# The first group's back product by seven products too, with the outputs of a chain left in its bank

## The chip, the cores and the metric

The kernel runs on one NeuronCore of a Trainium2 chip. The metric is the device time of one execution in microseconds; lower is better. Before the change three runs gave 863.26, 864.15 and 864.43 us, median 864.15. Engines: TensorE (PE) multiplies, ScalarE (ACT) copies and splits, VectorE (DVE) adds and subtracts, GpSimd (POOL) and SyncE (SP) issue transfers.

## What is computed

Three stages on 2304 tokens of 512 features, in float32:

```
x = attention(q, k, v)            # chunks of 64 tokens, 8 heads of 64
h = x @ w_in                      # 512 x 2048
y = (h * sigmoid(h)) @ w_out      # 2048 x 512      first MLP
a, b = y @ w_a, y @ w_b           # 512 x 1536      gated MLP
return (a * b) @ w_o2             # 1536 x 512
```

## The kernel before

**Precision.** [...] A product takes three passes: high by high, high by low, low by high. To split, ACT copies (the high part) and DVE subtracts (the low part).

**First MLP.** The weights come in a packed form and are unpacked in the course of the kernel. Blocks of 512 tokens go through 16 steps m of 128 hidden features. A step issues 12 matmuls of the next step's front (128x512), then 12 of its own back. SiLU runs on ACT, which writes `g` and its high part `ghi`; DVE makes `glo` (L409), which the back's third, sixth, ... matmul reads.

**Gated MLP.** Its tokens are three groups ("pairs") of two times T = 384. The front products are made by seven block products instead of eight (Strassen's scheme in Winograd's form): the weights' blocks are added and subtracted beforehand (`comb_sums`, L497: three DVE instructions) and split. One *unit* is one of the two matrices at one of STEPS = 6 steps: 7 products of 6 matmuls 128x384 each, gathered into four outputs. Pair 0 takes the combined weights while they are made: `make_half` (L522) splits products 0 to 3 of a unit (1024 wide) and 4 to 6 (768 wide) into a *ring* of 7 slots, from which they also leave for memory as `wg`. Later pairs read them back (`feed`, L553). `freed` or `refill` makes or fetches the next half when a half has been used.

The back by w_o2 is done by seven products in pairs 1 and 2, with combinations of w_o2 (`comb_load_2`, `comb_split_2`, L474 to L493). They are made once, four in the last A block (the steps of `W2_AT`) and two in pair 1, and are kept in memory as `w2`. In pair 0 the back is plain: 216 matmuls 128x512 (`back_b`, L694), three quarters of them in blocks of nine or twelve between the front products, with w_o2 split and stored high/low in the first MLP and loaded back by 24 transfers (`load_o2`, L1044).

**Order.** Every engine works its instructions in the order in which the program is written; there is no scheduler. Tiles come from pools with a fixed number of slots. The pool `big` has MA + 4 = 20 slots of 8 KB a partition and serves weights, ring, `buf` (loaded weights before their sums), `hl` (split combinations of w_o2 before they are written) and others; an instruction that writes a tile waits until the last reader of its slot is done, a transfer too. `in_last` (L1057) puts the work on weights into the 16 steps of the last A block, at two places of each ("c" and "c2"), ahead of that step's `glo`. `load_pair` (L587) brings y back for the operands of the next pair; for pair 0 that stands in step 5 of the last A block.

A chain of pair 0 (`chain`, L642) leaves its banks by four copies on ACT and four adds on DVE (`evacuate`, L1238, in the later pairs).

Of the kernel before, what the change touches and what calls it, by code (L numbers as in the profile page):

```python
# [20 lines left out]
P = 128  # L21
# [3 lines left out]
def chunk_attention_silu_mlp_gated_mlp(  # L25
# [10 lines left out]
    out: bass.AP,  # L36
# [26 lines left out]
    DM = out.shape[1]  # L63
# [57 lines left out]
    o2 = {}  # L121
# [67 lines left out]
    def upper():  # L189
        if not stage_1:  # L190
            return
        dest, w, sg, _ = stage_1.pop()
        nc.vector.scalar_tensor_tensor(  # L193
            out=w, in0=w, scalar=2.0**-20, in1=sg, op0=ALU.mult, op1=ALU.mult
        )
        if dest[0] == "f":
            wf[dest[1:]] = d = dram.tile([P, DM], F32, name=f"wf{dest[1]}{dest[2]}")
            leaving.append((d, w))
            return
        if dest[0] == "a":  # L200
            _, m, j = dest
            if m not in slots_a:
                slots_a[m] = slot("wA").rearrange("p (j n) -> p j n", j=4)
            hl = slots_a[m][:, 2 * j:2 * j + 2]
        else:
            wf[2, dest[1]] = d = dram.tile([P, DM], F32, name=f"wf2{dest[1]}")
            leaving.append((d, w))
            hl = late["conv"].tile([P, 2, DM], F32R, tag="hl", name="hl", bufs=1)
        nc.scalar.activation(hl[:, 0], w, AF.Copy)  # L209
        stage_2.append((dest, hl, w))  # L210

    def lower():
        if not stage_2:
            return
        dest, hl, w = stage_2.pop()
        nc.vector.tensor_tensor(out=hl[:, 1], in0=w, in1=hl[:, 0].bitcast(F32), op=ALU.subtract)
        if dest[0] == "a":
            wA.setdefault(dest[1], {})[dest[2]] = hl[:, 0], hl[:, 1]
        else:
            o2[dest[1]] = d = dram.tile([P, 2, DM], F32, name=f"wo{dest[1]}")  # L220
            leaving.append((d, hl.bitcast(F32)))
# [241 lines left out]
    def comb_load(u):  # L463
# [6 lines left out]
        for m, sl in ((2 * s, slice(1, 3)), (2 * s + 1, slice(0, 8, 4))):  # L470
# [3 lines left out]
    def comb_load_2(s):  # L474

        buf = slot("buf", F32).rearrange("p (o n) -> p o n", o=8)
        for h in range(2):
            nc.gpsimd.dma_start(out=buf[:, 1 - h], in_=wf[2, 2 * s][:, h * H:(h + 1) * H])
        nc.gpsimd.dma_start(
            out=buf[:, 2:6:2], in_=wf[2, 2 * s + 1].rearrange("p (o n) -> p o n", o=2)  # L480
# [16 lines left out]
    def comb_sums(u):  # L497
        summed.add(u)
        a21, a11, a12, s1, a22, s2, s4, s3 = (bufs[u][:, o] for o in range(8))
        nc.vector.tensor_tensor(out=s3, in0=a21, in1=a11, op=ALU.subtract)  # L500
        nc.vector.tensor_tensor(
            out=bufs[u][:, 3:6:2],
            in0=bufs[u][:, 0:8:7],
# [43 lines left out]
    for p in range(PAIRS):  # L547
        base.append(len(feeds))
        feeds += [wg[n] for n in range(2 * UNITS)]
        if p:  # L550
            feeds += [w2[:, n:min(n + 4, OPS * STEPS)] for n in range(0, OPS * STEPS, 4)]
# [11 lines left out]
    def chunk():  # L563
        u, o = divmod(used[0], OPS)
        h = int(o >= HALVES[1][0])
        return ring[2 * u + h][:, o - HALVES[h][0]]

    owed = [0]

    def chunk_done():  # L570
        used[0] += 1
        if used[0] % OPS in (0, HALVES[1][0]):
            owed[0] += 1
# [10 lines left out]
    pieces = []  # L584
# [16 lines left out]
    def operands(p):  # L601
# [4 lines left out]
        def take(o):  # L606
            if o not in xo:
# [3 lines left out]
                pieces.append(t[:, 2 * n:])  # L611
# [11 lines left out]
        def sub(dst, a, b):  # L623
# [4 lines left out]
            hi(0, b11), hi(5, b22), lo(0, b11), hi(1, b21), sub(t1, b12, b11),  # L628
            lo(5, b22), hi(2, t1), sub(t3, b12, b22), lo(1, b21), hi(6, t3), lo(2, t1),
            sub(t2, b22, t1), hi(4, t2), lo(6, t3), sub(t4, b21, t2), hi(3, t4),  # L630
            lo(4, t2), lo(3, t4),
        ]


    o2_at = {}
    gT2 = []

    order = ["at", "sB", "sA", "mm", "acc3"]

    held = []  # L640

    def chain(ct, filler):  # L642

        u0, u1, u2, u3, u4 = order
        order[:] = [u4, u1, u3, u2, u0]
        x1, x2, x3, x4 = (bank(t, [P, T]) for t in (u0, u2, u1, u3))

        def prod(ps, o, first):
            whi, wlo = (chunk()[:, i] for i in range(2))
            xhi, xlo = xo[o]  # L650
            for j, (a, b) in enumerate(((whi, xhi), (whi, xlo), (wlo, xhi))):
                for kk in range(KH):
                    nc.tensor.matmul(  # L653
                        ps,
                        lhsT=a[:, kk * P:(kk + 1) * P],
                        rhs=b[:, kk, :],
                        start=(first and j == 0 and kk == 0),
                        stop=(j == 2 and kk == KH - 1),
                        skip_group_check=True,
                    )  # L660
            chunk_done()

        def add(c, ps):
            nc.vector.tensor_tensor(out=ct[:, c], in0=ps, in1=ct[:, c], op=ALU.add)

        def keep(c, ps):
            nc.scalar.activation(ct[:, c], ps, AF.Copy)

        prod(x1, 0, True)
        keep(0, x1)  # L670
        prod(x3, 1, True)
        add(0, x3)
        refill()
        prod(x2, 2, True)
        keep(3, x2)
        prod(x4, 3, True)
        keep(2, x4)
        while held:
            held.pop()()
        yield  # L680
        prod(x1, 4, False)
        keep(1, x1)
        prod(x2, 5, False)
        add(1, x2)
        refill()
        yield
        filler()
        prod(x1, 6, False)
        add(2, x1)
        add(3, x1)  # L690

    accs = {}

    def back_b(t, m, ghi, glo, tag=None):  # L694

        if m == 0:
            accs[t] = bank(tag or f"acc{t}", [P, DM])
        whi, wlo = o2_at[m]
        for i, (g, w) in enumerate(((ghi, whi), (ghi, wlo), (glo, whi))):
            nc.tensor.matmul(  # L700
                accs[t],
                lhsT=g,
                rhs=w,
                start=(m == 0 and i == 0),
                stop=(m == MB - 1 and i == 2),
            )

    def store(p, t, by_act, halves=False):
        st = spool.tile([P, DM], F32, tag="tmp", name="ost", bufs=3)
        ps = accs.pop(t)  # L710
        if halves:
            nc.scalar.activation(st[:, :H], ps[:, :H], AF.Copy)
            nc.vector.tensor_copy(st[:, H:], ps[:, H:])
        elif by_act:
            nc.scalar.activation(st, ps, AF.Copy)
        else:
            nc.vector.tensor_copy(st, ps)
        r = (2 * NTB * p + t) * P
        (nc.scalar if by_act and not halves else nc.sync).dma_start(out=out[r:r + P, :], in_=st)

    g1 = {}

    def first_block(m0, mi):

        ghi, glo = g1.pop((m0, mi))
        for t in range(NTB):
            cols = slice(t * P, (t + 1) * P)
            back_b(t, m0 + mi, ghi[:, cols], glo[:, cols])

    def gate(ca, cb, s, c):  # L730

        m0, mi, second = 2 * s, c // 2, c % 2
        m = m0 + mi
        dst = gT2[m // 4][:, m % 4] if second else cb[:, c]
        nc.vector.tensor_tensor(out=dst, in0=ca[:, c], in1=cb[:, c], op=ALU.mult)

        def split():
            ghi = gpool.tile([P, T], F32R, tag="ghi", name="ghi")
            glo = gpool.tile([P, T], F32R, tag="glo", name="glo")
            nc.scalar.activation(ghi, dst, AF.Copy)  # L740
            nc.vector.tensor_tensor(out=glo, in0=dst, in1=ghi.bitcast(F32), op=ALU.subtract)
            g1[m0, mi] = ghi, glo

        return split

    def second_split(t, k, in_gpool):

        if in_gpool:
            hl = [gpool.tile([P, 4, P], F32R, tag=tg, name=tg) for tg in ("ghi", "glo")]
        else:  # L750
            if "gsp" not in late:
                late["gsp"] = spool.tile([P, 2, 2 * DM], F32R, tag="raw", name="gsp", bufs=1)
            half = late["gsp"][:, turn[0] % 2].rearrange("p (t m n) -> p t m n", t=2, m=4)
            turn[0] += 1
            hl = [half[:, 0], half[:, 1]]
        src = gT2[k][:, :, t * P:(t + 1) * P]
        nc.scalar.activation(hl[0], src, AF.Copy)
        nc.vector.tensor_tensor(out=hl[1], in0=src, in1=hl[0].bitcast(F32), op=ALU.subtract)
        return hl

    def second_back(t, k, hl, tag):
        for i in range(4):
            back_b(NTB + t, 4 * k + i, hl[0][:, i], hl[1][:, i], tag)
# [4 lines left out]
    for s in range(STEPS):  # L768
        for mat in range(2):
            units_b += [("f", mat, 2 * s), ("f", mat, 2 * s + 1), ("o", 2 * s + mat)]  # L770
# [20 lines left out]
    def prep_b():  # L791
        if done[1] < len(units_b):
            dest = units_b[done[1]]
            src = w_o2[dest[1]] if dest[0] == "o" else (w_a, w_b)[dest[1]][dest[2]]
# [15 lines left out]
    with tc.manual_schedule():  # L810
# [221 lines left out]
        o2_slots = []  # L1032
# [10 lines left out]

        def load_o2(m):  # L1044
            o2_at[m] = []
            for i in range(2):
                if not pieces and len(o2_slots) < 4:
                    o2_slots.append(slot("wo2"))
                    pieces.extend(o2_slots[-1][:, j * DM:(j + 1) * DM] for j in range(4))
                if pieces:  # L1050
# [448 lines left out]
```

## Time and profile before

| | |
|---|---|
| Median of three runs | 864.15 us |
| Profiled execution | 863.38 us |
| Its span, first to last instruction | 861.6 us |
| PE busy | 851.5 us (99%) |
| DVE busy | 588.7 us (68%) |
| ACT busy | 434.9 us (50%) |
| Granted clock of TensorE | 1.000 |

The span is what the trace covers; 1.8 us of the execution lie outside it. Durations are read from one execution, times of day in the trace count from the span's start. In a timeline a row "x6" is six instructions on end; the start of the next row less its own start is what a product takes, since matmuls overlap at their ends.

### The profile page before, as it was taken

The numbers are of one execution on the slowest core, as the hardware profiler recorded it, in microseconds if no ns is written. First come the engines' busy times: TensorE is split into PE (matmuls) and PEld (weight loads), VectorE is DVE, ScalarE is ACT, GpSimd is POOL, SyncE is SP. The second block draws the span as 40 slices with busy tenths as digits, with TensorE's granted clock in tenths as the row PEclk, the third lists the DMA queues.
The fourth block names the chain that finished last, engine by engine and source line by source line (L and its number), as shares of the span: only waits on it lengthen the run. The fifth ranks groups of instructions, "written<-read, shape, count | busy, mean of one in ns | idle before, by whom it ended". The sixth has DMA issues, their size and how long they took to land.

```text
span 861.6 us, 14197 instructions
## 1 busy us (share of the span) xinstructions
PE 851.5 (99%) x5448; PEld 767.9 (89%) x5448; DVE 588.7 (68%) x1143; ACT 434.9 (50%) x817; POOL 50.3 (6%) x91
## 2 busy tenths in 40 slices
PE   7999999999999999999999999999999999999998
PEld 7788888887888878888889999988999999999997
DVE  6997977757776577657575877445677686566663
ACT  6767766746664666544445443333334363333252
POOL 0000000020000000032200110000000000000000
PEclk9999999999999999999999999999999999999999
DMA  7354444266655665476984986654688887877751
GB/s 270 124 183 130 153 135 131 79 219 218 219 187 184 231 203 207 167 245 220 391 352 158 404 339 246 221 196 147 245 333 324 331 300 256 283 255 255 289 190 56
DMA packets 57347, 195.44 MB, mean 227 GB/s; under 512 B 6272, under 2 KB 12928, under 8 KB 50112
## 3 DMA queue, kind: packets, MB, share of 16 engines
q1 hardware_dynamic: 49632, 170.54, 55.0%
q0 software_dynamic: 6928, 22.81, 8.0%
q10 hardware_dynamic: 720, 1.18, 0.4%
q8 instruction: 43, 0.70, 0.3%
q14 instruction: 24, 0.20, 0.1%
HBM read 136.31 MB, written 58.20 MB: 226 GB/s over the span
## 4 chain that ended last, share of the span: by engine, by line
PE 97%; ACT 1%; DVE 1%; DMA 1%; SPq 0%; issue 0%; DVEq 0%; ACTq 0%
PE ps_acc L431 21%; PE ps_acc L1233 15%; PE ps_mm L392 15%; PE ps_sA L392 7%; PE ps_at L1233 7%; PE ps_acc L700 5%; PE ps_sA L1233 4%; PE ps_sB L653 2%; PE ps_sA L653 2%; PE ps_at L653 2%; PE ps_sB L1233 2%; PE ps_mm L1233 2%; PE ps_acc L653 2%; PE ps_sA L431 2%; PE ps_mm L653 1%; PE ps_sB L431 1%
## 5 line engine op out<-in xcount | busy, mean ns | idle before, releaser
L431 PE MATMUL ps_acc<-ghi,wA 128*128 128x512 f32 x512 | 159.9, 394 | 0.0
L1233 PE MATMUL ps_acc<-xo,ring 128*128 128x384 f32 x582 | 111.5, 334 | 0.0
L431 PEld LDWEIGHTS ps_acc<-ghi,wA 128*128 128x128 f32 x512 | 93.8, 188 | 19.2
L1233 PEld LDWEIGHTS ps_acc<-xo,ring 128*128 128x128 f32 x582 | 101.9, 188 | 0.0
L392 PE MATMUL ps_mm<-xhi,wA 128*128 128x512 f32 (+1 forms) x400 | 100.7, 373 | 0.0
L431 PE MATMUL ps_acc<-glo,wA 128*128 128x512 f32 x256 | 100.0, 391 | 0.0
L392 PEld LDWEIGHTS ps_mm<-xhi,wA 128*128 128x128 f32 x400 | 70.5, 188 | 12.6 <-ACT wA L209 0.2
L412 ACT ACTIVATE g<-ps_mm 128x512 f32<-128x512 f32 (+1 forms) x50 | 28.0, 560 | 86.7 <-PE ps_mm L392 81.7
L409 DVE TENSOR_TENSOR glo<-g,ghi 128x512 fp32r<-128x512 f32 x80 | 50.5, 632 | 19.1 <-ACT ghi L413 19.1
L1246 ACT ACTIVATE gq<-ps_acc 128x384 f32<-128x384 f32 x56 | 27.6, 492 | 60.2 <-PE ps_acc L1233 57.5
L431 PEld LDWEIGHTS ps_acc<-glo,wA 128*128 128x128 f32 x256 | 48.0, 188 | 10.3
L153 ACT ACTIVATE e<-e,ebias 128x512 uint16<-128x512 uint16 x68 | 49.1, 722 | 5.5 <-DVE e L150 5.5
L1233 PE MATMUL ps_at<-xo,ring 128*128 128x384 f32 x252 | 51.1, 334 | 0.0
L1284 DVE TENSOR_TENSOR u<-gq,u 128x384 fp32r<-128x384 f32 x56 | 29.7, 555 | 30.5 <-ACT u L1283 30.2
L392 PE MATMUL ps_mm<-xlo,wA 128*128 128x512 f32 (+1 forms) x200 | 49.8, 371 | 0.0
L392 PE MATMUL ps_sA<-xhi,wA 128*128 128x512 f32 x184 | 49.6, 391 | 0.0
L1243 DVE TENSOR_TENSOR gq<-ps_acc,gq 128x384 f32<-128x384 f32 x56 | 29.9, 554 | 26.0 <-PE ps_acc L1233 25.1
L193 DVE SCALAR_TENSOR_TENSOR mant<-mant,sg 128x512 f32<-128x512 f32 x68 | 46.6, 685 | 0.1
L174 DVE SCALAR_TENSOR_TENSOR mant<-raws,mant 128x512 f32<-128x512 uint32 x68 | 46.6, 685 | 0.1
L149 ACT ACTIVATE sg<-raws 128x512 bf16<-128x512 bf16 x68 | 45.8, 674 | 0.7 <-DMA raws<-w_in 0.7
L373 DVE TENSOR_TENSOR xlo<-ps_at,xhi 128x256 fp32r<-128x256 f32 (+1 forms) x13 | 6.8, 527 | 56.1 <-ACT xhi L369 56.1
L1233 PEld LDWEIGHTS ps_at<-xo,ring 128*128 128x128 f32 x252 | 44.4, 188 | 0.2
(221 smaller groups left out, 1715.9 us busy)
## 6 DMA issues: line engine op xcount, KB each, us to landing
ring<-wg SPq DMA_DIRECT2D x24, 1024.0 KB, 5.6
ring<-w SPq DMA_DIRECT2D x20, 1024.0 KB, 4.8
ring<-wg SPq DMA_DIRECT2D x24, 768.0 KB, 5.0
wg<-ring SPq DMA_DIRECT2D x12, 1024.0 KB, 9.5
wf<-mant SPq DMA_DIRECT2D x36, 256.0 KB, 3.0
wg<-ring SPq DMA_DIRECT2D x12, 768.0 KB, 9.7
raws<-w_in SPq DMA_DIRECT2D x16, 512.0 KB, 3.5
raws<-w_out SPq DMA_DIRECT2D x16, 512.0 KB, 3.5
```

The lines of the kernel that those rows point to most:

```text
L149: nc.scalar.activation(sg, topb, AF.Sign)
L153: nc.scalar.activation(e, e, AF.Relu, scale=8.0, bias=ebias)
L174: nc.vector.scalar_tensor_tensor(out=mant, in0=w32[:, :, 0], scalar=2.0**-32, in1=mant.bitcast(U32), op0=ALU.mult, op1=ALU.add,)
L193: nc.vector.scalar_tensor_tensor(out=w, in0=w, scalar=2.0**-20, in1=sg, op0=ALU.mult, op1=ALU.mult)
L392: nc.tensor.matmul(ps, lhsT=a[:, kk * P:(kk + 1) * P], rhs=b[:, kk, :], start=(j == 0 and kk == 0), stop=(j == 2 and kk == KT - 1),)
L409: nc.vector.tensor_tensor(out=glo, in0=g, in1=ghi.bitcast(F32), op=ALU.subtract)
L431: nc.tensor.matmul(acc_t[b][j], lhsT=a[:, j * P:(j + 1) * P], rhs=g, start=(m == 0 and i == 0 and (b != SIDE or j % 2 == 0)), stop=(m == M ...
L653: nc.tensor.matmul(ps, lhsT=a[:, kk * P:(kk + 1) * P], rhs=b[:, kk, :], start=(first and j == 0 and kk == 0), stop=(j == 2 and kk == KH - ...
L700: nc.tensor.matmul(accs[t], lhsT=g, rhs=w, start=(m == 0 and i == 0), stop=(m == MB - 1 and i == 2),)
L1233: nc.tensor.matmul(ps, lhsT=a, rhs=b, start=first and i == 0, stop=last and i == 2, skip_group_check=True,)
L1243: nc.vector.tensor_tensor(out=ct[c], in0=ps, in1=ct[c], op=ALU.add)
L1284: nc.vector.tensor_tensor(out=lo, in0=src, in1=hi.bitcast(F32), op=ALU.subtract)
```

## The change

All three pairs now run the same code, and the whole output is written transposed (`out_t`). The plain back with its splits, loads and stores is gone. All six combinations of w_o2 are made in the last A block (steps 3 to 8).

A chain gathers differently: the seven products go into three banks, A, B, A, E, A, B, A, and products 2, 4 and 6 are added by TensorE onto what the bank holds. After each product the bank is copied or added out, so four outputs need four copies on ACT and three adds on DVE; in odd units the last goes from the bank straight into the gate's multiplication. Two chains run interleaved. In round u the order is: product 0 of unit u, product 4 of unit u-1, 1 of u, 5 of u-1, 2 of u, 6 of u-1, 3 of u. Banks are taken in rotation from all eight.

```diff
-        W2_AT = [3, 4, 5, 6]
+        W2_AT = [3, 4, 5, 6, 7, 8]
...
-            if m > 12:
-                load_o2(m - 13)
...
+        BANK = "ABAEABA"
+        FRESH = (0, 1, 3)
+
+        def evacuate(o, ps, ct):
+
+            act, c = ((keep, 0), (keep, 3), (keep, 1), (add, 0), (add, 3), (add, 1), (keep, 2))[o]
+            act(ct[c], ps)
...
+        def front_product(p, u, o):
+            if o == 0:
+                open_chain(p, u)
+            ps, ct = chains[p, u]
+            if o in FRESH:
+                ps[BANK[o]] = next_bank()
+            x = ps[BANK[o]]
...
+            if o == OPS - 1 and u % 2:
+                gate(p, u // 2, 2, x)
+            else:
+                evacuate(o, x, ct)
+            if o in (HALVES[1][0] - 1, OPS - 1):
+                freed()
...
-        for p in range(1, PAIRS):
+        for p in range(PAIRS):
...
+            for u in range(1, UNITS):
+                s = (u - 1) // 2
+                front_product(p, u, 0)
+                if u % 2 == 0:
+                    gate(p, s, 0)
+                elif s:
+                    split(s - 1, 1, gq[s - 1][0])
+                front_product(p, u - 1, 4)
+                if u % 2 == 0:
+                    gate(p, s, 3)
+                front_product(p, u, 1)
+                if u % 2 == 0:
+                    first_operand(p, s)
+                front_product(p, u - 1, 5)
+                if u % 2 == 0:
+                    gate(p, s, 1)
+                    second_operand(s)
+                front_product(p, u, 2)
+                front_product(p, u - 1, 6)
+                front_product(p, u, 3)
```

DVE in pair 0's front, before, some two units in the middle: `ring` rows are the low parts of a ring half, L500 begins the three sums, L664 adds a bank to an output, L735 is the gate, L741 a split.

```order
L532 TENSOR_TENSOR ring_5421<-buf_5293,ring_5421 128x4x256
L735 TENSOR_TENSOR cb_5326<-ca_5325,cb_5326 128x384
L664 TENSOR_TENSOR cb_5326<-ps_sA_5404,cb_5326 128x384
L532 TENSOR_TENSOR ring_5454<-buf_5293,ring_5454 128x3x256
L500 TENSOR_TENSOR raws_82<-raws_82 128x256
L501 TENSOR_TENSOR raws_82<-raws_82 128x2x256
L507 TENSOR_TENSOR raws_82<-raws_82 128x256
L735 TENSOR_TENSOR g2_5324<-ca_5325,cb_5326 128x384
L741 TENSOR_TENSOR glo_5466<-cb_5326,ghi_5465 128x384
L664 TENSOR_TENSOR cb_5326<-ps_sB_5403,cb_5326 128x384 x2
```

The same engine and place now, from an even round into an odd one; L945 is the add of a bank to an output, L1006 the gate, L1092 the double subtract, L1060 a split, L521 the ring, L489 to L496 the sums.

```order
L945 TENSOR_TENSOR gq_5133<-ps_sA_5151,gq_5133 128x384
L1006 TENSOR_TENSOR gq_5133<-gq_5133,ca_5057 128x384
L1092 TENSOR_TENSOR gq_5133<-gq_5133 128x768
L1006 TENSOR_TENSOR gq_5133<-ps_sB_5134,ca_5057 128x384
L521 TENSOR_TENSOR ring_5254<-raws_82,ring_5254 128x4x256
L945 TENSOR_TENSOR ca_5202<-ps_acc2_5258,ca_5202 128x384
L521 TENSOR_TENSOR ring_5266<-raws_82,ring_5266 128x3x256
L489 TENSOR_TENSOR buf_5199<-buf_5199 128x256
L490 TENSOR_TENSOR buf_5199<-buf_5199 128x512
L496 TENSOR_TENSOR buf_5199<-buf_5199 128x256
L1060 TENSOR_TENSOR u_5228<-gq_5133,u_5228 128x384
L945 TENSOR_TENSOR ca_5202<-ps_acc0_5203,ca_5202 128x384
```

The last row is the add of product 4 (bank A, here `acc0`), on which product 6 of the same unit waits; both halves of the ring and the sums now stand between it and the gates of the step before.

DVE in the last A block before, steps 7 and 8: `glo` (L409) of the next step stands behind a ring half.

```order
L409 TENSOR_TENSOR glo_4655<-g_4653,ghi_4654 128x512
L500 TENSOR_TENSOR buf_4519<-buf_4519 128x256
L501 TENSOR_TENSOR buf_4519<-buf_4519 128x2x256
L507 TENSOR_TENSOR buf_4519<-buf_4519 128x256
L532 TENSOR_TENSOR ring_4695<-buf_4519,ring_4695 128x4x256
L409 TENSOR_TENSOR glo_4689<-g_4687,ghi_4688 128x512
L532 TENSOR_TENSOR ring_4699<-buf_4519,ring_4699 128x3x256
```

The same place now; `hl` (L478) is the split of a combination of w_o2, `buf_4527` the sixth of them.

```order
L478 TENSOR_TENSOR hl_4617<-buf_4466,hl_4617 128x3x256
L489 TENSOR_TENSOR buf_4459<-buf_4459 128x256
L490 TENSOR_TENSOR buf_4459<-buf_4459 128x512
L496 TENSOR_TENSOR buf_4459<-buf_4459 128x256
L521 TENSOR_TENSOR ring_4654<-buf_4459,ring_4654 128x4x256
L489 TENSOR_TENSOR buf_4527<-buf_4527 128x256
L490 TENSOR_TENSOR buf_4527<-buf_4527 128x512
L496 TENSOR_TENSOR buf_4527<-buf_4527 128x256
L478 TENSOR_TENSOR hl_4660<-buf_4527,hl_4660 128x4x256
L398 TENSOR_TENSOR glo_4648<-g_4646,ghi_4647 128x512
L521 TENSOR_TENSOR ring_4665<-buf_4459,ring_4665 128x3x256
L478 TENSOR_TENSOR hl_4669<-buf_4527,hl_4669 128x3x256
```

Three sums and the larger split of the sixth combination have moved in front of step 9's `glo`; ACT's part of that split takes the slot that the third combination's smaller split held.

## Rows read from the trace of the kernel before

**Rows 1.** The page's engine table: busy us, share of the span, instructions.

```profile
PE 851.5 (99%) x5448; PEld 767.9 (89%) x5448; DVE 588.7 (68%) x1143; ACT 434.9 (50%) x817; POOL 50.3 (6%) x91
```

**Rows 2.** Table by stage: stretch, us, busy us of each engine, clock, DMA.

```profile
core 0: us, PE busy (x) PEld busy (x) DVE busy (x) ACT busy (x) POOL busy (x), PEclk, DMA share, GB/s
454.56:589.10 134.54, 134.54 (x709) 125.95 (x708) 87.90 (x149) 54.95 (x98) 10.55 (x17) 1.00 0.67 251
589.10:725.97 136.87, 136.87 (x782) 135.84 (x781) 92.88 (x167) 55.43 (x111) 1.80 (x3) 1.00 0.78 288
725.97:861.60 135.63, 131.41 (x757) 131.09 (x756) 79.52 (x150) 45.20 (x98) 0.00 (x0) 1.00 0.65 226
400.00:425.00 25.00, 25.00 (x112) 20.71 (x111) 16.44 (x24) 10.40 (x16) 5.08 (x8) 1.00 1.05 382
```

**Rows 3.** PE's timeline: start, us, engine, line, operation; pair 0's back inside pair 1.

```profile
596.07 2.94 PE L700 MATMUL ps_acc<-wo,gsp 128*128 128x512 f32 x12
598.85 1.23 PE L1233 MATMUL ps_at<-xo,ring 128*128 128x384 f32 x6
```

**Rows 4.** Timeline at the span's end.

```profile
856.18 1.20 PE L1233 MATMUL ps_acc<-u,ring 128*128 128x384 f32 x6
857.42 1.02 DVE L1243 TENSOR_TENSOR gq<-ps_acc,gq 128x384 f32<-128x384 f32 x2 [2.12 <-PE ps_acc L1233]
```

**Rows 5.** DVE's timeline in pair 0's front.

```profile
506.60 0.56 DVE L664 TENSOR_TENSOR cb<-ps_sA,cb 128x384 f32<-128x384 f32 x1 [2.00 <-PE ps_sA L653]
507.07 0.95 DVE L532 TENSOR_TENSOR ring<-buf,ring 128x768 fp32r<-128x768 f32 x1
507.94 0.42 DVE L500 TENSOR_TENSOR raws<-raws 128x256 f32<-128x256 f32 x1
508.39 0.69 DVE L501 TENSOR_TENSOR raws<-raws 128x512 f32<-128x512 f32 x1
509.11 0.43 DVE L507 TENSOR_TENSOR raws<-raws 128x256 f32<-128x256 f32 x1
509.46 0.55 DVE L735 TENSOR_TENSOR g<-ca,cb 128x384 f32<-128x384 f32 x1
...
521.68 1.22 DVE L532 TENSOR_TENSOR ring<-buf,ring 128x1024 fp32r<-128x1024 f32 x1
522.82 0.55 DVE L735 TENSOR_TENSOR cb<-ca,cb 128x384 f32<-128x384 f32 x1
```

**Rows 6.** ACT's timeline there: copy of a bank, then a ring half.

```profile
520.10 0.49 ACT L667 ACTIVATE cb<-ps_sB 128x384 f32<-128x384 f32 x1 [4.00 <-PE ps_sB L653]
520.49 1.06 ACT L531 ACTIVATE ring<-buf 128x1024 fp32r<-128x1024 f32 x1
```

**Rows 7.** Line L471, the loads of weights for the sums: their transfers.

```profile
DMA to landing us min/median/max: 4.8/6.8/11.8
```

**Rows 8.** Timelines of the last A block; last, line L493 (writes of `w2`), 410 to 422.

```profile
400.76 0.85 ACT L488 ACTIVATE hl<-buf 128x768 fp32r<-128x768 f32 x1 [1.10 <-DMA w<-hl]
409.49 1.79 ACT L488 ACTIVATE hl<-buf 128x1024 fp32r<-128x1024 f32 x2
420.37 1.79 ACT L531 ACTIVATE ring<-buf 128x1024 fp32r<-128x1024 f32 x2
...
406.88 0.95 DVE L489 TENSOR_TENSOR hl<-buf,hl 128x768 fp32r<-128x768 f32 x1
411.72 0.68 DVE L409 TENSOR_TENSOR glo<-g,ghi 128x512 fp32r<-128x512 f32 x1
...
406.92 8.27 SPq L596 DMA_DIRECT2D yr<-y  x6
415.28 5.50 SPq L493 DMA_DIRECT2D w<-hl  x3
...
425.09 0.39 PE L431 MATMUL ps_acc<-glo,wA 128*128 128x512 f32 x1
...
DMA to landing us min/median/max: 10.0/10.2/11.1
```

More of the change, by code (lines that the diff above doesn't have):

```diff
@@ L199, in upper @@
             return
[L200 to L208, printed above, removed]
+        _, m, j = dest
+        if m not in slots_a:
+            slots_a[m] = slot("wA").rearrange("p (j n) -> p j n", j=4)
+        hl = slots_a[m][:, 2 * j:2 * j + 2]
         nc.scalar.activation(hl[:, 0], w, AF.Copy)
@@ L498, in comb_sums @@
         summed.add(u)
-        a21, a11, a12, s1, a22, s2, s4, s3 = (bufs[u][:, o] for o in range(8))
+        a21, a11, s1, s2, a12, s3, s4, a22 = (bufs[u][:, o] for o in range(8))
         nc.vector.tensor_tensor(out=s3, in0=a21, in1=a11, op=ALU.subtract)
         nc.vector.tensor_tensor(
-            out=bufs[u][:, 3:6:2],
-            in0=bufs[u][:, 0:8:7],
+            out=bufs[u][:, 2:4],
+            in0=bufs[u][:, 0:6:5],
             in1=a22.unsqueeze(1).to_broadcast([P, 2, H]),
@@ L627, in operands @@
         return [
[L628 to L631, printed above, removed]
-        ]
[L635 to L759, printed above, removed]
@@ L1041, in enter_b @@
             load_pair(0)
[L1044 to L1050, printed above, removed]
-                    d = pieces.pop(0)
-                else:
-                    d = late["b"].tile([P, DM], F32R, tag="wo2", name="wo2")
-                nc.sync.dma_start(out=d.bitcast(F32), in_=o2[m][:, i])
-                o2_at[m].append(d)
         def in_last(m, pos):
@@ L1090, in end_last, with next_bank, triple @@
                 first.extend(operands(0))
-            if m > 12:
-                load_o2(m - 13)
-        def pair_tiles():
-            return [late["b"].tile([P, 4, T], F32, tag=tg, name=tg) for tg in ("ca", "cb")]
+        BANKS = ("at", "sB", "sA", "mm", "acc0", "acc1", "acc2", "acc3")
+        taken = [0]
+        def next_bank():
+            t = bank(BANKS[taken[0] % len(BANKS)], [P, T])
+            taken[0] += 1
+            return t
+        def triple(ps, w, x, first, last):
+            (whi, wlo), (xhi, xlo) = w, x
+            for i, (a, b) in enumerate(((whi, xhi), (whi, xlo), (wlo, xhi))):
+                nc.tensor.matmul(
+                    ps, lhsT=a, rhs=b, start=first and i == 0, stop=last and i == 2,
+                    skip_group_check=True,
+                )
@@ new lines, in add, with keep, open_chain @@
+        def add(dst, ps):
+            nc.vector.tensor_tensor(out=dst, in0=ps, in1=dst, op=ALU.add)
+        def keep(dst, ps):
+            nc.scalar.activation(dst, ps, AF.Copy)
+        BANK = "ABAEABA"
[3 more added lines that the diff above has]
+            act(ct[c], ps)
+        gq = []
+        gflat = []
+        oc = []
+        units = []
+        chains = {}
+        def open_chain(p, u):
+            s = u // 2
+            if u % 2:
+                if p == 0:
+                    t = slot("gq", F32)
+                    gflat.append(t[:, :4 * T].rearrange("p (c n) -> p c n", c=4))
+                    gq.append([gflat[s][:, c] for c in range(4)])
+                    oc.append(t[:, 4 * T:5 * T])
+                ct = gq[s]
+            else:
+                t = late["b"].tile([P, 4, T], F32, tag=("ca", "cb")[s % 2], name="ca")
+                ct = [t[:, c] for c in range(4)]
+            chains[p, u] = {}, ct
@@ new lines, in front_product @@
+        def front_product(p, u, o):
[5 more added lines that the diff above has]
+            x = ps[BANK[o]]
+            h = int(o >= HALVES[1][0])
+            w = ring[base[p] + 2 * u + h][:, o - HALVES[h][0]]
+            for kk in range(KH):
+                triple(
+                    x,
+                    [w[:, i, kk * P:(kk + 1) * P] for i in range(2)],
+                    [a[:, kk] for a in xo[o]],
+                    o in FRESH and kk == 0,
+                    kk == KH - 1,
+                )
+            if o == OPS - 1 and u % 2:
+                gate(p, u // 2, 2, x)
+            else:
+                evacuate(o, x, ct)
+            if o in (HALVES[1][0] - 1, OPS - 1):
+                freed()
@@ L1097, in chunk_attention_silu_mlp_gated_mlp, with gate, begin_round @@
+        def gate(p, s, c, ps=None):
+            nc.vector.tensor_tensor(
+                out=gq[s][c],
+                in0=gq[s][c] if ps is None else ps,
+                in1=chains[p, 2 * s][1][c],
+                op=ALU.mult,
+            )
+        def begin_round(p):
+            for o in (0, 1, 3, 2):
+                front_product(p, 0, o)
         for k in range(END):
@@ L1223, in chunk_attention_silu_mlp_gated_mlp @@
-        gq = []
-        half = OPS // 2 + 1
-        def freed():
-            owed[0] += 1
-            refill()
-        def triple(ps, w, x, first, last):
-            (whi, wlo), (xhi, xlo) = w, x
-            for i, (a, b) in enumerate(((whi, xhi), (whi, xlo), (wlo, xhi))):
-                nc.tensor.matmul(
-                    ps, lhsT=a, rhs=b, start=first and i == 0, stop=last and i == 2,
-                    skip_group_check=True,
-                )
-        def evacuate(o, x, ct):
-            x1, x3, x2, x4 = x
-            def add(c, ps):
-                nc.vector.tensor_tensor(out=ct[c], in0=ps, in1=ct[c], op=ALU.add)
-            def keep(c, ps):
-                nc.scalar.activation(ct[c], ps, AF.Copy)
-            (
-                lambda: keep(0, x1),
-                lambda: add(0, x3),
-                lambda: keep(3, x2),
-                lambda: keep(2, x4),
-                lambda: keep(1, x1),
-                lambda: add(1, x2),
-                lambda: (add(2, x1), add(3, x1)),
-            )[o]()
@@ L1258, in chunk_attention_silu_mlp_gated_mlp @@
-        SETS = (("at", "sB", "sA", "mm"), ("acc0", "acc1", "acc2", "acc3"))
-        BANK = (0, 1, 2, 3, 0, 2, 0)
-        def front_chain(p, u, ct, tags):
-            x = [bank(t, [P, T]) for t in tags]
-            ct = [ct[:, c] for c in range(4)]
-            for o in range(OPS):
-                h = int(o >= half)
-                hi, lo = (ring[base[p] + 2 * u + h][:, o - half * h, i] for i in range(2))
-                for kk in range(KH):
-                    w = [a[:, kk * P:(kk + 1) * P] for a in (hi, lo)]
-                    triple(x[BANK[o]], w, [a[:, kk] for a in xo[o]], o < 4 and kk == 0, kk == KH - 1)
-                evacuate(o, x, ct)
-                if o in (half - 1, OPS - 1):
-                    freed()
-                yield
@@ L1309, in take_units, with minus, first_operand, second_operand @@
                 )
-        def minus(s, c, a, b, op=ALU.subtract):
-            nc.vector.tensor_tensor(out=gq[s][c], in0=gq[s][a], in1=gq[s][b], op=op)
-        def settle(s):
-            split(s, 1, gq[s][2])
+        def minus(s, c, a, b):
+            nc.vector.tensor_tensor(out=gq[s][c], in0=gq[s][a], in1=gq[s][b], op=ALU.subtract)
+        def first_operand(p, s):
+            if p == 0:
+                take_units(s)
+            split(s, 0, gq[s][0])
+        def second_operand(s):
             nc.vector.tensor_tensor(
@@ L1393, in make @@
                 del new[:n]
-            x = [[bank(t, [P, T]) for t in tags] for tags in SETS]
-            ct = [[oc[j], oc[j], oc[4 + j], oc[2 + j]] for j in range(2)]
+            x = [{}, {}]
+            ct = [[oc[j], oc[2 + j], oc[j], oc[4 + j]] for j in range(2)]
             def back(o, s, j):
+                if o in FRESH and s == 0:
+                    x[j][BANK[o]] = next_bank()
                 n = STEPS * o + s
@@ L1406, in done @@
             def done(o, j):
[L1407 to L1427 removed]
+                evacuate(o, x[j][BANK[o]], ct[j])
+                if o > 2:
+                    c = (0, 3, 1, 2)[o - 3]
+                    store_t(p, j, c, ct[j][c], nc.scalar if last and c == 2 else nc.sync)
+            s, u = STEPS - 1, UNITS - 1
+            gate(p, s, 0)
+            split(s - 1, 1, gq[s - 1][0])
+            front_product(p, u, 4)
+            gate(p, s, 3)
+            for i in range(3):
+                back(0, i, 0)
+            first_operand(p, s)
+            front_product(p, u, 5)
+            gate(p, s, 1)
+            second_operand(s)
+            for i in range(3):
+                back(0, i, 1)
+            front_product(p, u, 6)
+            split(s, 1, gq[s][0])
+            for j in range(2):
+                for i in range(3, STEPS):
+                    back(0, i, j)
+            for i in range(STEPS):
+                minus(i, 0, 3, 0)
+            for j in range(2):
+                done(0, j)
+            for o in range(1, OPS - 1):
+                for i in range(STEPS):
+                    for j in range(2):
+                        back(o, i, j)
+                for i in range(STEPS):
+                    split(i, o % 2 ^ 1, gq[i][(0, 2, 1, 3, 2)[o - 1]])
+                    if o == 4:
+                        minus(i, 2, 2, 0)
                 for j in range(2):
@@ L1430, in chunk_attention_silu_mlp_gated_mlp @@
                 if o >= 2:
-                    make(4)
+                    make(5)
             for j in range(2):
-                for s in range(STEPS):
-                    back(OPS - 1, s, j)
+                for i in range(STEPS):
+                    back(OPS - 1, i, j)
                 done(OPS - 1, j)
```

211 lines of the change are left out of this document (21 added, 190 removed).

## The prediction

> **What bounds the kernel now.** I read the engine table of the page first, then the table by stage, then TensorE's timeline, and only then the two engines behind it. TensorE (PE) is busy for 851.5 of 861.6 us [rows 1]: whatever it does not issue any more is won, and whatever makes it wait is lost. [...] The last stage has 4.2 us without PE behind its last matmul. The ends of the last A block's weight work and the DMA queue (1.05 of its share at 382 GB/s) come last in the reading, because they matter only when an instruction is queued in front of one that PE needs.
>
> **Matmuls.** One product is six matmuls 128x384. Pair 1 goes from 589.10 to 725.97 and holds two groups of twelve 128x512 matmuls that belong to pair 0's back, 596.07 to 598.85 = 2.78 us each [rows 2, 3]: 136.87 - 5.56 = 131.31 us for 756 matmuls of 384, 1.042 us a product. Pair 0 takes 134.54 us to pair 1's first product, plus these 5.56, minus the last A step's twelve matmuls that lie in it (as many and as wide, 2.78): 137.32 us. By seven products it has the 756 matmuls of pair 1, 131.31 us. **Term 1: -6.01 us.** Pairs 1 and 2 already stand at that pace without a gap, so the second interleaving and the lighter DVE give them nothing, unless they break something: 0.
>
> **Tail.** After the last matmul DVE takes up two adds at 857.42 for 1.02 us [rows 4]; after the change one ACT copy, 0.49 us [rows 6], is left before the last store. **Term 2: -0.55 us** (0 to -0.6).
>
> **Pair 0's front.** Removed on DVE: one of four adds a unit, and the w_o2 splits. Taken away on PE, too: the blocks of 9 matmuls of the plain back, which stood in every unit and gave DVE time. A unit is now seven products, 7.30 us. What DVE must do does not shrink that much, since the ring halves (hi/lo of the combined weights) are made here as before, until round 8. The new point is a short deadline: product 4 of a unit leaves its bank by the add into output 3, and product 6 of the same unit writes that bank again three products later (3.1 us). This add stands in DVE's row behind ring halves, sums and a split, as the order shows. From start to start of neighbours [rows 5]: 384 add, gate or split 0.47 us; ring half of 1024 1.14; of 768 0.87, and the double subtract, as wide, the same; the three sums 0.45 + 0.72 + 0.35 = 1.52; an instruction that needs its neighbour's result starts 0.03 after its end rather than 0.09 before it, 0.12 more.
> Odd rounds (3, 5, 7), from one such add to the next: 8 x 0.47 + 0.87 (double) + 1.14 + 0.87 + 1.52 = 8.16, with three dependent neighbours 8.52, where PE has 7.30 us of products. PE waits 1.22 us (0.86 without those three).
> Even rounds (2, 4, 6, 8): here DVE catches up, but the row begins with the ring half that ACT makes behind the copy of product 6. From the end of product 6: 0.20 until an engine takes it up [rows 4], copy 0.39 and ring 1.06 on ACT [rows 6], 0.05, then on DVE 1.14 + 0.47 + 0.87 + 1.52 + gate 0.47 + add 0.55, and 0.06 to PE: 6.78, against six products 6.25. PE waits 0.53.
> **Term 3: 3 x 1.22 + 4 x 0.53 = +5.8 us.** Bounds: 0, if ACT and DVE start earlier than their rows follow from PE, which nothing in the rows says, to about +10 (late loads, below). I take the sum.
> The neighbours' overlap counts here: 506.60 + 0.56 ends 0.09 after the next start at 507.07 [rows 5]; without it an odd round would cost a microsecond more.
>
> **Last A block.** Six instead of four combinations of w_o2 are made here: their splits (ACT 1.06 us for the larger part, DVE 1.23) at steps 7 and 8, 1 MB more loads, 3.5 MB more writes; 12 writes of hi/lo w_o2 go, most of them earlier. Work in this block's slack costs PE nothing in itself; before carries the same at steps 3 to 6. But ACT's split of step 8 needs a slot of the big pool, and the pool's 20 are taken: the slot is one from which an earlier combination (the third's smaller part) is still being written. The chip shows such a wait once already: ACT idle 1.10 us before 400.76, for a write of hl [rows 8]. The split that held the slot was through DVE at 407.8, but its write stands on SP behind six loads of yr that take 8.27 us to issue: it is issued at 415.28 and the landings of those three writes take 10.0 to 11.1 us, so 425.3 [rows 8]. With half a MB net more in the full queue at 382 GB/s, +1.3: 426.6. Behind the split on DVE stands glo of step 9, which PE uses at 425.09 [rows 8]. From the ACT start of such a split to the end of glo is 409.49 to 411.72 + 0.68 = 2.91 us [rows 8]: 429.5, 4.4 us late. The next split and ring half wait for the other two writes, which by then have mostly landed: 0 to 1 us at step 10, 0.6 taken. **Term 4: +5.0 us.** Bounds: +0.8 if the write lands early (then only 1.14 of split in front of glo is left, of which 0.3 finds room), 8.5 if each of the later splits waits as well.
> [...]
>
> **Other edits.** The 24 loads of w_o2 and the output stores of 128x512 leave SP's queue; the queue had lookahead to spare, 0. The back's splits and subtracts lie under six times twelve matmuls (2.08 us each), with 93 us of DVE on 137 in pair 1 now [rows 2]: 0, and up to +1 if the next pair's operands are late. Eight banks in rotation instead of two sets of four: each comes back more than a unit later, 0.
>
> **Sum:** -6.01 - 0.55 + 5.8 + 5.0 = +4.2 on the profiled execution's 863.38: 867.6. That execution lies 0.77 under the median of 864.15; 868.4 against the median.
>
> **The rivals.**
> 1. Both waits stay away: PE waits only for the product before. -6.6 us: 857.6. For it: PE is busy in all 134.54 us of pair 0, DVE in 65% of them [rows 2]. Against it: rooms of 2.08 us in each unit go with the plain back.
> 2. One of the two happens. Only pair 0's: -6.56 + 5.8 + 0.8 = 0, 864.2. Only the A block's: -6.56 + 5.0 = -1.6, 862.6. The first if the write lands by 421.4, when ACT is through the first ring half of 420.37 [rows 8]; the second if DVE's odd round takes under 7.3 us.
> 3. Both, and the loads of the combined weights come late (slower side). A buffer that is free after its 768 half is loaded anew, and its sums stand one round later in the row: 7.9 us less some 0.4. Landing is 4.8 / 6.8 / 11.8 us least, median, most [rows 7], on a unit of 9.4 us (seven products and nine 512 matmuls). From 7.5 us each microsecond later costs up to 1 us in the rounds 3 to 8; at 9 us some +4: 872.4. Against it: the queue carries less in pair 0, since 24 loads are gone.
>
> **Chances.** Forecast 0.48, rival 1 0.14, rival 2 0.21 (half each), rival 3 0.17. What a measurement of this kernel tells from no change is about 0.2%, 1.7 us. Rival 1 is faster; of rival 2 0.12 no change, 0.06 faster, 0.03 slower; of the forecast 0.45 slower, 0.03 none; rival 3 slower: 0.20, 0.15, 0.65. The forecast's own range is 865.5 to 871, from 0.86 to 1.22 in odd rounds and 2.5 to 7 in the A block. The wide range, 860.5 to 874, leaves out most of rival 1 and the worst of rival 3.
>
> **What shows it.** Right: PE idle some 4 us near 425 with DVE glo as its releaser, behind an ACT split that waited for a write of the combined w_o2; in pair 0 seven idles of 0.5 to 1.3 us, PE released by the add of output 3, alternately larger and smaller, none after round 8; pair 0's matmuls 131.3 us without them. Wrong: a PE without idle between 416 and 560 (rival 1), idle before DVE's sums released by DMA (rival 3), or gaps in pairs 1 and 2.

## The result

The changed kernel takes 874.91 us (median of four runs, 873.52 to 877.93) against 864.29 us before (four runs): ratio 1.013, 95% interval 1.010 to 1.016. It is slower, by 10.6 us where 4.2 were forecast, and just outside the wide range of 860.5 to 874. The profiled execution is the longest of the four, 877.93 us with a span of 876.2. In it the start-up, whose code the change doesn't touch, ends 2.97 us later than before (first back of the first MLP at 37.04 against 34.07); in the profiles of the nine further kernels below, which share this code, the point lies between 34.20 and 35.16. So at least 1.9 of these 3 us belong to this execution; I leave all 3 out of the account of the change.

### The profile page after: what moved, and what is told of

It is laid out like the page before. It is cut to its first block, busy times and chain, and to the rows that moved or that the text cites. A ratio compares the mean times of both kernels' runs of the same rounds, so it can differ in the third digit from the quotient of the medians.

```text
span 876.2 us, 14154 instructions
## 1 busy us (share of the span) xinstructions
PE 853.0 (97%) x5484; PEld 773.5 (88%) x5484; DVE 579.5 (66%) x1124; ACT 431.0 (49%) x816; POOL 52.2 (6%) x91
## 4 chain that ended last, share of the span: by engine, by line
PE 82%; DVE 9%; DMA 3%; issue 2%; ACT 2%; SPq 0%; POOL 0%; ACTq 0%; DVEq 0%
PE ps_acc L420 18%; PE ps_acc L939 18%; PE ps_mm L381 13%; PE ps_sA L381 6%; PE ps_at L939 5%; PE ps_sB L939 5%; PE ps_mm L939 4%; PE ps_sA L939 4%; DMA buf<-wf 2%; PE ps_sA L420 2%; PE ps_sB L420 1%; DVE u L1060 1%; PE ps_at L381 1%; DVE ring L521 1%; PE ps_at L267 1%
## 5 line engine op out<-in xcount | busy, mean ns | idle before, releaser
L939 PE MATMUL ps_acc<-xo,ring 128*128 128x384 f32 x864 | 167.8, 335 | 2.5 <-DVE ca L945 1.9
L939 PEld LDWEIGHTS ps_acc<-xo,ring 128*128 128x128 f32 x864 | 151.2, 188 | 3.8 <-DVE ca L945 2.5
L1060 DVE TENSOR_TENSOR u<-gq,u 128x384 fp32r<-128x384 f32 x87 | 46.1, 552 | 30.3 <-ACT u L1059 30.3
L939 PE MATMUL ps_acc<-u,ring 128*128 128x384 f32 x270 | 52.8, 337 | 2.9 <-ACT u L1059 1.9
L1059 ACT ACTIVATE u<-gq 128x384 fp32r<-128x384 f32 x87 | 42.1, 516 | 22.5 <-DVE gq L1092 12.4
L948 ACT ACTIVATE gq<-ps_acc 128x384 f32<-128x384 f32 x42 | 20.7, 492 | 65.5 <-PE ps_acc L939 65.4
L939 PEld LDWEIGHTS ps_acc<-u,ring 128*128 128x128 f32 x270 | 47.3, 188 | 4.0 <-ACT u L1059 2.6
L939 PE MATMUL ps_at<-xo,ring 128*128 128x384 f32 x231 | 47.8, 334 | 0.0
```

The lines of the kernel that those rows point to most:

```text
L939: nc.tensor.matmul(ps, lhsT=a, rhs=b, start=first and i == 0, stop=last and i == 2, skip_group_check=True,)
L948: nc.scalar.activation(dst, ps, AF.Copy)
L1059: nc.scalar.activation(hi, src, AF.Copy)
L1060: nc.vector.tensor_tensor(out=lo, in0=src, in1=hi.bitcast(F32), op=ALU.subtract)
```

## The profile after

The engine table, as [rows 1]:

```profile
PE 853.0 (97%) x5484; PEld 773.5 (88%) x5484; DVE 579.5 (66%) x1124; ACT 431.0 (49%) x816; POOL 52.2 (6%) x91
```

The table by stage, as [rows 2]: the last A block, pairs 0, 1 and 2 (stretch, us, busy us of each engine, clock, DMA).

```profile
376.63:465.71 89.08, 83.35 (x359) 67.92 (x357) 58.49 (x87) 40.57 (x60) 20.28 (x32) 0.98 0.84 312
465.71:607.95 142.24, 136.68 (x769) 133.36 (x768) 106.00 (x183) 62.50 (x119) 9.66 (x14) 1.00 0.73 270
607.95:741.18 133.23, 131.79 (x758) 131.22 (x757) 77.24 (x138) 47.96 (x100) 0.00 (x0) 1.00 0.75 272
741.18:876.20 135.02, 131.42 (x757) 131.09 (x756) 67.79 (x127) 44.07 (x94) 0.00 (x0) 0.99 0.61 224
```

PE is no longer busy without a break: 5.7 us are missing in the A block, 5.6 in pair 0, 1.4 in pair 1. Its timeline shows where. First the A block:

```profile
427.43 0.80 PE L420 MATMUL ps_acc<-glo,wA 128*128 128x512 f32 x1 [4.67 <-DVE glo L398]
428.03 1.05 PE L420 MATMUL ps_acc<-ghi,wA 128*128 128x512 f32 x2
435.77 0.50 PE L420 MATMUL ps_acc<-glo,wA 128*128 128x512 f32 x1 [1.04 <-DVE glo L398]
```

then pair 0's front, an even and an odd round, of seven such rows (four of 0.33, three of 0.92 to 0.95; the last at 534.87, round 8), and its back:

```profile
485.66 1.33 PE L939 MATMUL ps_mm<-xo,ring 128*128 128x384 f32 x6 [0.34 <-DVE gq L945]
494.16 1.32 PE L939 MATMUL ps_acc<-xo,ring 128*128 128x384 f32 x6 [0.92 <-DVE ca L945]
...
600.79 0.44 PE L939 MATMUL ps_acc<-u,ring 128*128 128x384 f32 x1 [0.96 <-ACT u L1059]
601.71 1.16 PE L939 MATMUL ps_acc<-u,ring 128*128 128x384 f32 x5 [0.48 <-DVE u L1060]
```

The last pair of rows comes back in pair 1 (734.06), and not in pair 2, which makes no operands for a next pair. Behind each wait the second matmul starts 0.1 us late as well. From start to start of matmuls, less the pace (0.174 us a matmul), so with this late start and the overlap that is lost: pair 0's front 6.0 us (4 x 0.60 + 3 x 1.20), the back 1.98 us in each of two pairs.

In the A block there is more than idle. ACT, DVE and the clock around it, and the write's transfer time (line L482, the one issued at 409.34):

```profile
417.32 0.43 DVE L496 TENSOR_TENSOR buf<-buf 128x256 f32<-128x256 f32 x1
...
424.46 1.79 ACT L477 ACTIVATE hl<-buf 128x1024 fp32r<-128x1024 f32 x2 [6.47 <-DMA buf<-wf]
...
425.55 1.22 DVE L478 TENSOR_TENSOR hl<-buf,hl 128x1024 fp32r<-128x1024 f32 x1 [7.80 <-ACT hl L477]
426.69 0.68 DVE L398 TENSOR_TENSOR glo<-g,ghi 128x512 fp32r<-128x512 f32 x1
...
426.00:428.00 2.00, 0.57 (x1) 0.50 (x2) 2.00 (x3) 1.22 (x3) 0.00 (x0) 0.85 1.07 389
428.00:430.00 2.00, 2.00 (x6) 1.59 (x5) 1.70 (x4) 0.61 (x1) 0.00 (x0) 0.50 1.05 407
430.00:432.00 2.00, 2.00 (x8) 1.60 (x8) 1.52 (x2) 0.45 (x1) 0.00 (x0) 0.79 1.05 408
...
DMA to landing us min/median/max: 15.0/15.0/15.0
```

ACT starts 0.1 us after that write lands (409.34 + 15.0); the releaser that the profile prints, a load, is another transfer of that moment. The split's own source had been there for long: DVE's sums of the fifth combination, which read it, end at 417.75. After 4.7 us without a matmul the granted clock stands at 0.50 for some 3.5 us, and a 512 matmul takes 0.427 us instead of 0.227: the ten matmuls from 427.43 to 431.39 take 3.96 us instead of 2.27, 1.7 us more. From the first back matmul of step 8 to pair 0's first product the kernel before and the first experiment take 35.4 us, the changed kernel 43.56: **8.2 us**, 5.7 of them idle and 1.7 the clock.

How late that write lands changes from execution to execution, and PE's first idle with it. Four kernels run the same program up to this point and through the A block (this one and experiments 2, 3 and 5): the write takes 15.0, 13.5, 12.3 and 15.3 us to land, and PE's idle before the `glo` of step 8 is 4.67, 3.17, 1.92 and 4.99 us, each time the landing less 10.3 us. So this write has 10.3 us of room. In the kernel before it took 9.7 us (landed at 416.06), and in experiments 1, 4, 8 and 9, where the loads of the last two combinations (1 MB) go out later, 9.8 to 10.2. What makes it late is these loads in the queue.

The account of this execution: -6.0 (matmuls) - 0.7 (tail) + 8.2 (A block) + 6.0 (pair 0's front) + 4.0 (back of pairs 0 and 1) = 11.5, with 3.0 of start-up 14.5 of the 14.6 us by which the spans differ (876.2 - 861.6).

## The experiments

The kernel before was timed again with each series and took 863.82 to 864.09 us there, so the times can be set beside one another.

**1. The last two combinations later.**

```diff
-        W2_AT = [3, 4, 5, 6, 7, 8]
+        W2_AT = [3, 4, 5, 6]
+        W2_LATE = [11, 15]   # sums and both splits at "c2"
...
```

> The fifth and sixth combination of w_o2 are made at steps 11 and 15 of the last A block, behind that step's glo, instead of steps 7 and 8. Theory (ACT's split of step 7 waits for a slot whose write is still in a full queue, glo stands behind it, and the long wait lowers the clock): the idle of 4.7 and 1.0 us before glo near 427 and 436 goes, and with it the stretch at a granted clock of 0.5 behind it; 8 us less than the changed kernel, some 867. Rival (the queue is full anyway, the next ring half then waits as long): 3 us or more of idle stay near 425, and the time is 870 or more.

868.4 us, 6.5 less than the changed kernel of the 8 forecast. PE and clock in the A block:

```profile
420.00:430.00 10.00, 10.00 (x45) 8.27 (x45) 6.17 (x9) 5.53 (x8) 3.24 (x5) 1.00 1.06 402
430.00:440.00 10.00, 10.00 (x46) 8.27 (x45) 7.42 (x12) 4.79 (x7) 0.00 (x0) 1.00 1.03 423
```

PE is full, the clock 1.00, with the DMA as busy as ever (share 1.03 to 1.06): here the full queue cost PE nothing, since nothing that PE needed waited for it. The stretch is 35.36 us. A wait of 0.7 us (0.56 of it idle, at 465.41) came in at pair 0's first products.

**2. Four operands a stage.** `make(5)` becomes `make(4)` in the back.

> The back hands out the next pair's operands four at a time behind products 2 to 5 instead of five. Theory (an ACT copy of an operand waits for a DVE subtract and holds up the splits for product 6 behind it): the idle of 1.0 and 0.5 us before product 6 of pairs 0 and 1 goes, 3.9 us less than the changed kernel, some 871. Rival (DVE simply has more to do in the stage of product 5, with six more subtracts there, than the stage lasts): the wait stays at 1 us or more a pair, or comes back at the next pair's first products; 873 to 875.

871.71 us, 3.2 less. In pair 0's back 0.30 us of idle are left of 1.4:

```profile
596.41 1.15 PE L939 MATMUL ps_acc<-u,ring 128*128 128x384 f32 x5 [0.30 <-DVE u L1060]
```

Pair 1 goes from 133.23 to 131.83 us, pair 0 from 142.24 to 140.78. So 2.9 us are the operand's. The two medians say less: their runs overlap (871.22 to 874.30 against 873.52 to 877.93), since the A block's stretch, 42.09 us in this profile, changes with the execution.

**3. The sums on GpSimd.** `nc.vector` becomes `nc.gpsimd` in `comb_sums` for the ring units of pair 0.

> The three sums of each ring unit in pair 0's front go to GpSimd instead of DVE. Theory (DVE's row between two adds of output 3 is longer than seven products): odd rounds need 8.5 - 1.5 = 7.0 of 7.3 us, even ones 6.8 - 1.5 = 5.3 of 6.25, so all seven idles of 0.3 to 1.0 us go, 6 us less than the changed kernel, some 869. Rival 1 (the adds are late because of ACT's ring half or late loads): the idles stay, 874. Rival 2 (GpSimd at work makes DVE's instructions longer, or its sums come too late for the ring half): DVE's 384 forms over 0.6 us, or idle before ring halves released by GpSimd, 872 or more.

870.13 us, 4.8 less. Pair 0 takes 137.09 us, 5.2 less; of the seven waits two small ones are left. The theory on DVE's row holds. The second rival holds in part, as the next run shows.

**4. All three.**

> The three edits together (late combinations, four operands, sums on GpSimd). Theory: the three waits are separate and their prices add up, 8 + 3.9 + 6 = 18 us less than the changed kernel, 857, which is the 6.6 us under the kernel before that the matmuls and the tail are worth. Rival: a wait that goes at one place comes back at the next, 862 or more.

863.22 us, ratio to before 0.998 (0.997 to 1.000): 857 was missed. The A block is 35.36 us, pair 1 131.85, but pair 0 138.9, with two idles of 1.4 us. DVE and GpSimd ahead of the first:

```profile
495.54 1.19 DVE L522 TENSOR_TENSOR ring<-raws,ring 128x768 fp32r<-128x768 f32 x1
496.65 1.63 DVE L1069 TENSOR_TENSOR u<-gq,u 128x384 fp32r<-128x384 f32 x1
498.20 1.01 DVE L954 TENSOR_TENSOR ca<-ps_acc,ca 128x384 f32<-128x384 f32 x2
...
495.18 0.73 POOL L490 TENSOR_TENSOR buf<-buf 128x256 f32<-128x256 f32 x1 [2.71 <-DMA buf<-wf]
495.99 1.87 POOL L491 TENSOR_TENSOR buf<-buf 128x512 f32<-128x512 f32 x1
```

A split that takes 0.55 us alone takes 1.63 beside GpSimd's sum, and it stands in front of the add that PE needs. The adds, which read a bank and one tile, stay at 0.55. In experiment 3 the split at this place took 1.09 us and PE waited 0.16: how much it costs seems to depend on when GpSimd's sum, which waits for a load, comes to stand beside it.

**5. The sums behind the adds, on DVE.** In odd rounds `comb_sums` is held back until the adds of products 4 and 5 are issued:

```diff
+                hold[0] = u % 2 == 0
                 front_product(p, u, 3)
...
                 front_product(p, u - 1, 5)
+                while sums_due:
+                    comb_sums(sums_due.pop())
```

> The changed kernel, but in odd rounds of pair 0's front the three sums stand on DVE behind the adds of products 4 and 5 instead of in front of them; nothing goes to GpSimd and no work is left out. Theory (in odd rounds it is the length of DVE's row up to the add of output 3 that counts): that row is 8.5 - 1.5 = 7.0 us against 7.3, the three idles of 0.9 us go and the four of 0.3 us in even rounds stay, 3.6 us less than the changed kernel, some 871. Rival (DVE is short of time as a whole, wherever the sums stand): the idles move to the even rounds, or to idle before product 6 of the odd rounds behind, and the time stays within 1.5 us of 874.

871.47 us, 3.4 less; pair 0 takes 139.10 us, 3.1 less than in the changed kernel. All waits of pair 0's front:

```profile
483.83 1.31 PE L941 MATMUL ps_mm<-xo,ring 128*128 128x384 f32 x6 [0.34 <-DVE gq L947]
499.53 1.31 PE L941 MATMUL ps_sB<-xo,ring 128*128 128x384 f32 x6 [0.87 <-DVE gq L947]
514.70 3.42 PE L941 MATMUL ps_acc<-xo,ring 128*128 128x384 f32 x18 [0.34 <-DVE gq L947]
529.90 1.33 PE L941 MATMUL ps_acc<-xo,ring 128*128 128x384 f32 x6 [0.34 <-DVE gq L947]
```

The three odd waits are gone, the four even ones stand (one of them 0.5 longer, for a load that came 0.44 us late to DVE). The same work, only in another order: what counts is the length of the row in front of the add.

**6. The loads of y later.** `load_pair(0)` moves from step 5 to step 9 of the last A block.

> The changed kernel, but the loads of y for pair 0's operands go out at step 9 of the last A block instead of step 5; all six combinations stay at steps 3 to 8. Theory (the split of step 7 waits for the write of the third combination's larger part, which shares the queue with the loads of y): that write lands some 4 us or more earlier than 15 us after its issue, the idle of 4.7 us before glo shrinks to 0 to 2 us and the clock doesn't fall; 4 to 7 us less than the changed kernel, 868 to 871. Rival (the idle is for the split's own source, loaded by GpSimd, as the profile's releaser says; or the writes themselves fill the queue): it stays above 3 us, 873 or more.

875.1 us: nothing gained. ACT at step 7:

```profile
421.10 1.06 ACT L477 ACTIVATE hl<-buf 128x1024 fp32r<-128x1024 f32 x1 [5.10 <-DMA w<-hl]
```

The write still takes 13.6 us (15.0 in the changed kernel), PE's first idle is 3.3 us and its second 1.6 instead of 1.0. The three writes behind it go out earlier and take 13.1 to 14.5 us. The theory on y fails: the queue is full with weights and writes alone (DMA share 1.03 to 1.04 from 405 to 420). What holds ACT up is named here as the write: it lands at 421.00, and ACT starts at 421.10.

**7. glo in front.** The fifth and sixth combination stay at steps 7 and 8, but stand behind that step's `glo` (position "c2").

> The changed kernel, with the fifth and sixth combination still at steps 7 and 8 of the last A block, but their sums and splits behind that step's glo instead of in front of it; loads, writes and slots are as before. Theory (the price is that glo stands behind an instruction that waits for a write; the wait itself may stay): ACT still waits some 6 us before the split of step 7, PE's idle of 4.7 us at glo of step 8 goes, up to 2 us of idle come at the next step, since ACT's ghi and the ring half are late there, and the granted clock stays at 1.00: 4 to 7 us less than the changed kernel, 868 to 871. Rival (the late write is paid wherever the split stands, because the ring halves and ghi behind it on ACT are late by as much): 4 us or more of idle one step later, 873 or more.

875.92 us: PE waits as long as the rival says, one step later.

```profile
426.82 1.79 ACT L520 ACTIVATE ring<-buf 128x1024 fp32r<-128x1024 f32 x2 [6.20 <-DMA w<-hl]
```

Here the split finds its slot in time (417.05), and the first ring half waits for a slot whose write (the third combination's smaller part) lands at 426.72; PE then waits 4.4 us one step later. The edit does more than was expected of it: at "c2" the load of a later unit's weights stands ahead of the split and asks for a slot before it, so the slots go to other tiles than in the changed kernel. It shows that the slots have their price with `glo` in front of the split too: an instruction on ACT that asks for a slot whose tile is still being written holds up all behind it. What glo's place alone is worth, with the slots as they were, no run shows.

**8 and 9. Versions made of these.** Both have late combinations, four operands, the six subtracts of the back in the stage of product 3 and the odd rounds' split behind the adds; 8 has the sums on GpSimd, 9 on DVE as in experiment 5.

> Late combinations, four operands, sums on GpSimd, and two edits more: the split of odd rounds stands behind the adds of products 4 and 5, and the six subtracts of the back stand in the stage of product 3. Theory (what was left with the three edits is one long split, slowed by GpSimd, in front of the add of output 3, and 0.5 us a pair in the back): the two idles of 1.4 us and the two of 0.3 us go, 3 to 4.5 us less than with the three edits, 859 to 860. Rival (GpSimd's slowing of DVE then shows at another instruction): the sum of the idles stays at 2 us or more, 862 or more.

> As the run before, but the sums stay on DVE, in odd rounds behind the adds. Theory: no slowing by GpSimd; only the four even idles of 0.3 us are left, with the restart behind them 2.4 us: 859 to 861. Rival (the ring half on DVE comes too late behind the moved sums and split): odd idles of 0.5 us or more come back, 863.

Version 8 takes 859.36 us, as forecast, ratio to before 0.994 (0.993 to 0.996), the fastest here; version 9 862.28 us, 0.998 (0.997 to 0.999). So version 8 is 0.6% faster than the kernel before. In version 8 pair 0 takes 135.47 us and PE is full again but for 0.7 us of idle in pairs 0 and 1 together:

```profile
PE 847.3 (99%) x5484; PEld 771.3 (90%) x5484; DVE 573.8 (67%) x1100; ACT 430.6 (50%) x816; POOL 81.5 (10%) x115
...
454.79:590.26 135.47, 135.02 (x769) 133.40 (x768) 103.43 (x164) 64.42 (x121) 37.16 (x39) 1.00 0.81 300
590.26:722.07 131.81, 131.59 (x758) 131.17 (x757) 77.21 (x139) 47.95 (x101) 0.00 (x0) 1.00 0.75 275
```

In version 9 the even waits and 0.7 us at pair 0's first products stay; its forecast of 859 to 861 was missed by 1.3 us. The two idles of 1.4 us are gone in version 8, where GpSimd still makes the sums but the split stands behind the add.

## Why the prediction was wrong

- **Matmuls, -6.01: right.** Pair 0's 142.24 us less 2.78 of A-block matmuls, 6.0 and 2.0 of waits are 131.5, pair 1's pace.
- **Tail, -0.55: nearly right, -0.7.** From the last matmul's start to the span's end 3.90 us against 4.57.
- **Pair 0's front, +5.8: right, 6.0, in part by luck.** Places, alternation and the end at round 8 are as forecast, and what a wait costs from start to start too: even 0.60 for 0.53, odd 1.20 for 1.22. The idles themselves are 0.33 and 0.92 to 0.95, shorter than the 0.5 to 1.3 us that were to show it. In even rounds the row was reckoned 0.2 us too long, and the lost overlap and late start of the matmuls behind a wait (0.27 us), for which there was no term, made up for it. Experiment 5 shows the odd term by itself, 3 and 5 together that it is the row and not the ring's loads. Rival 3's late loads did not come.
- **Last A block, +5.0: mechanism right, place and size off, 8.2.** The step that failed is which write ACT waits for. The forecast has only the third combination's smaller part, asked for at step 8, and gives the half MB more in the queue 1.3 us. The larger part is no term in it: before, it landed at 416.06, in time. With the loads of two more combinations in the queue it took 15.0 us where it has 10.3 of room, so the wait came one step earlier, at step 7. And there was no term for the clock: 1.7 us of matmuls at a granted clock of 0.50. That glo stands behind the split is not the price by itself: in experiment 7, with other slots asked for, the next slot's wait cost as much.
- **Other edits, 0 to +1 for the back: wrong, 4.0.** This is the largest error against what was forecast, and the prediction itself had named gaps in pair 1 as a sign of being wrong. The step that failed: I laid the splits and subtracts of a product under "six times twelve matmuls", 12.5 us, and it is six times six, 6.25 us. In the stage of product 4 the six splits, six subtracts, two adds and four of the five operands' instructions meet on DVE, 14 x 0.47 + 4 x 0.87 = 10.1 us (591.07 to 601.11); ACT, in order, holds the splits for product 6 behind an operand copy that waits for DVE. The profile shows the blocker and what stands behind it:

```profile
599.48 0.84 ACT L597 ACTIVATE xo<-yr 128x768 fp32r<-128x768 f32 x1 [6.37 <-DVE yr L605]
600.23 0.92 ACT L1059 ACTIVATE u<-gq 128x384 fp32r<-128x384 f32 x2
```

Sum of the forecast +4.2, of the measured terms in the profiled execution +11.5; the median moved by 10.6. The A block's stretch varies between executions (41.8 to 43.9 us in the four kernels that have it unchanged), and this profile is near the upper end.

## What to carry to other kernels

Before a block of filler work goes, write out for each in-order engine the row in front of the instruction that TensorE waits for, stage by stage; an engine at 75% of a long stretch can still be late at every second deadline. Work that is moved into a stretch with a full DMA queue (share 1.02 to 1.06 here) pays through the slots that it takes, and moving it on to later steps (6.5 us here) did what reordering it in place did not (nothing). Ask of each slot how late its write may land (10.3 us here) and not only how long the write took before. A wait on TensorE like the one of 4.7 us here is to be priced with the matmuls at the lower clock behind it (0.50 here, 1.7 us).

## What the runs showed of the hardware

- In the changed kernel the granted clock stood at 0.50 for some 3.5 us behind an idle of 4.67 us (0.50 from 428 to 430, 0.79 from 430 to 432, 1.00 from 432), and at 1.00 behind one of 1.04. In experiment 6 it was 0.83 from 420 to 430, behind an idle of 3.3 us, which is 3.4 us at 0.50, and 1.00 from 430 to 440, behind one of 1.6. It went to 0.50 also behind the idles of 3.2 us in experiment 2, 5.0 in 5 (there for nearly 7 us) and 4.4 in 7 (mean granted clock of the span 0.996, 0.994 and 0.996); in experiment 3 it stayed at 1.00 behind idles of 1.9 and 2.7 us (mean 0.999). In experiment 7 a second idle, of 2.1 us, was followed by some 3.5 us at 0.50 as well, so the length of the last idle alone does not tell.
- DVE instructions that read two tiles of SBUF were stretched while GpSimd ran sums (experiments 3, 4 and 8), from 0.55 to 1.09 or 1.63 us for 128x384; those that read PSUM and one tile were not (0.54 to 0.55 us there).
- The same write of 1 MB took 5.2 us to land for the first combination (issued at 398.46, when the queue had just begun to fill: DMA share 0.11 from 395 to 400) and 15.0 for the third (409.34, share 1.02 to 1.06 from 410 to 425).
